# A feed-forward layer behind window attention on one core: the second layer of two blocks as seven block products, with the sums of w_out made on chip

## The chip, the core and the metric

The kernel runs on one core of a Trainium2 chip. A core has TensorE (PE in the profile, its weight loads PEld), which multiplies matrices from SBUF into the eight banks of PSUM, VectorE (DVE), ScalarE (ACT) and GpSimd (POOL) for work on elements, and SyncE (SP), which here only issues DMAs; ScalarE and GpSimd issue DMAs too. Each engine works off its own list of instructions in order and waits on semaphores for the others. The metric is the time of one execution in microseconds of device time, the median of the runs.

## The reference

Attention with a causal window of 64 keys, and behind it a feed-forward layer with a leaky rectifier. All is float32.

```python
# q, k, v: (8, 8, 576, 64); w_in: (512, 2048); w_out: (2048, 512)
scores = scale * np.matmul(q, k.transpose(0, 1, 3, 2))
mask = (rel >= 0) & (rel < window)
scores = np.where(mask, scores, -1000000000.0)
attn = np.exp(scores - np.max(scores, axis=-1, keepdims=True))
attn = attn / (np.sum(attn, axis=-1, keepdims=True) + 1e-09)
x = np.matmul(attn, v)          # then laid out as (4608 tokens, 512)
h = x @ w_in
g = np.maximum(0.01 * h, h)
return g @ w_out
```

## The kernel before

The 4608 tokens are nine chunks of 512. The first three are done beside the attention in the plain way: h = x w_in in blocks of 128 columns (L853), g, and g w_out into accumulators (L862). The other six are three blocks, s = 0, 1, 2, of two chunks (t = 0, 1) each. To keep float32's precision, each operand is split into a high part that TensorE takes as it is and the remainder (the low part), and a product is three matmuls: high by high, high by low, low by high.

The first layer of a block (L1006, tiles m) is done as a 2 x 2 scheme of seven products in place of eight (a Strassen-like scheme): sums and differences of x (made by `x_build`, L788) by sums and differences of w_in (made once by the loop at L935: fetch two single-precision pieces from DRAM, four sums on VectorE, a split, two stores to `w_first` in DRAM). For each of 8 values of f there are seven products of 6 matmuls; VectorE and ScalarE put them together into four parts of g (L1012 to L1018). The second layer (L1031, tiles y) is the plain product: for each t and each of 16 f, ScalarE and VectorE split g into a pair of tiles (L1021, L1024; 512 columns, four pairs in rotation) and TensorE does four output tiles i by three matmuls of 512 columns into four PSUM banks, o0 to o3: 2 x 16 x 4 x 3 = 384 matmuls a block. `put_out` (L1033) evicts the banks, and SyncE stores them.

The weights of both layers come from DRAM by `fill` (L991), a GpSimd DMA of 1 MB into one of four ring tiles, which is issued when TensorE has left the tile. Late attention (`attend` and `normalise`, L734 and L758) goes on beside block 0 and the beginning of block 1: scores (L267), mask (L648), maximum across partitions on GpSimd (L657), subtraction (L664), exponential (L668), sum on GpSimd (L660), values (L704). The pairs of units are numbered m, 16 of them late (m from 20).

The order of each engine's instructions is decided at build time by a planner, `arrange` (L519): each step has a duration, the steps that it waits for, and a rank, and on each engine the step of lowest rank that is ready goes next. The numbers in it are the author's estimates; only the order that comes out reaches the chip. The first part of the program, up to some 130 us, is in an order written out by hand (L52); it also converts the 64-bit weights to single precision (L194 to L240) and stores the pieces of w_in (`split`, L232) for the preparation.

Buffer names in the profile: p, pfew, pxa, pxb are SBUF places that are used again and again, gs is a pair of tiles for the split g, e, late_e and late_f hold scores in rotation, g (as a VectorE operand of L664) the maxima, late_o the sums.

Of the kernel before, what the change touches and what calls it, by code (L numbers as in the profile page):

```python
# [24 lines left out]
P = 128  # L25
# [57 lines left out]
RING_AT = (5, 6, 7, 8)  # L83
KT = DM // P
# [14 lines left out]
def band_attention_ffn(ctx: ExitStack, tc: tile.TileContext, qT, kB, vW, vL, w_in, w_out, eye_mask, out, outT):  # L99
# [24 lines left out]
    vs = [const.tile([P, UNITS, 544], F32, name="v")]  # L124
    unit = const.tile([P, P], F32R, name="unit")
# [20 lines left out]
    def v_of(m):  # L146
        if m >= PAIRED:
            return vs[0][:, :, : H * D]
        return vs[m % 2 if m < TURNED // 2 else 0][:, :, : H * (D + 1)]
# [35 lines left out]
    w_single = dram.tile([FT, P, 512], F32, name="w_single")  # L185
    w_first = dram.tile([P, half * 7 * 512], F32, name="w_first")
    w_second = dram.tile([half, P, 2, 1024], F32, name="w_second")
# [45 lines left out]
    def split(n):  # L233
        nc.scalar.copy(flat(parts(n)[0]), singles[n])
        if n % 2 == 0:
            nc.scalar.dma_start(w_single[n // 2], singles[n])
# [159 lines left out]
    def open_room():  # L396

        e, n, f = (wk.tile([P, 512, 2], U32, tag="raw", bufs=3, name=f"late_{x}") for x in "enf")
# [175 lines left out]
    def g_part(t, f):  # L574
        n = 2 * t + f // half
        return g_tile(f % half)[:, 512 * n : 512 * (n + 1)]
# [50 lines left out]
    for f in turn_of:  # L627
# [4 lines left out]
        to = w_second[f // 2, :, f % 2].rearrange("p (i c) -> p i c", i=2)  # L632
        stored.append((f, partial(store, to, f, slice(None), slice(2, 4))))
# [8 lines left out]
    def shield_of(m, j):  # L642
# [4 lines left out]
        e, s = (x.rearrange("a (b c) -> a b c", c=n * QB) for x in (e_of(m)[:, j], ps))  # L647
        nc.vector.scalar_tensor_tensor(e, s, SCALE, a, ALU.mult, ALU.add)  # L648

# [12 lines left out]
    def minus_of(m, j):  # L662
        e = e_of(m)[:, j]
        nc.vector.tensor_tensor(e, e, most_of(j), ALU.subtract)  # L664
# [7 lines left out]

    def inverse_of(m):
        c = later["c"][m % 2]
        nc.vector.tensor_scalar_add(c, c, 1e-9)
# [58 lines left out]
    def attend(m, gate):  # L734
# [8 lines left out]
        takes = [before["take"], two["take"]] if m == EARLY else ()  # L743
# [3 lines left out]
        )  # L747
        for j in range(2):
            o[f"E{j}"] = op("DVE", ONE, partial(shield_of, m, j), o["S"], three.get("V"), three.get(f"A{j}"), gate, before.get("E1"), rank=0.8 + late)
        for j in range(2):  # L750
            o[f"P{j}"] = op("POOL", 1.95, partial(max_of, m, j), o[f"E{j}"], before.get(f"B{j}"), rank=0.5 + late)
            o[f"B{j}"] = op("DVE", TWO, partial(minus_of, m, j), o[f"P{j}"], rank=0.8 + late)
# [5 lines left out]
    def normalise(m):  # L758
# [3 lines left out]
        if "v" in o and before:  # L762
            o["v"]["after"].append(before["V"])
        o["I"] = op("DVE", 0.4, partial(inverse_of, m), o["c0"], o["c1"], rank=0.8 + late, lag=0.3 + 6 * late)
# [23 lines left out]
    def x_build(s, n, xt_at, xt_free, x_free):  # L788

        urge = 1.0 if s else 0.2  # L790
        m = (UPC * LEAD + 2 * UPC * s) // UNITS + 2 * n

        def raw():
            return g_tile(xt_at[0])[:, :1024].rearrange("p (i q c) -> p i q c", i=2, q=4)

        def sums():
            return g_tile(xt_at[1])[:, 1024 * (s == 0) :][:, :1024].rearrange("p (k i c) -> p k i c", k=4, i=2)
# [4 lines left out]
        def fetch(i):  # L802
            nc.sync.dma_start(g_tile(xt_at[0])[:, 512 * i : 512 * (i + 1)], x_rows[m + i])
# [6 lines left out]
        d = op("DVE", 0.5, partial(sub, 4, 0, 2), *got, rank=urge, lag=3 * urge - 0.4)  # L810
        d3 = op("DVE", 0.5, partial(sub, 6, 1, 0), *got, rank=urge, lag=3 * urge - 0.4)
# [14 lines left out]
        for a, b, after in ((0, 2, got), (2, 3, got), (3, 7, [d, d2, d3, d4])):  # L826
            hi = op("ACT", 0.2 + 0.213 * (b - a), lambda a=a, b=b: nc.scalar.copy(x_view(0, a, b), source(a, b)), *after, *x_free, rank=urge, lag=3 * urge - 0.4)
# [107 lines left out]
    for f in range(half):  # L935
        def prep(i, f=f):
            return g_tile(PREP_AT + f % 2).rearrange("p (k i c) -> p k i c", k=4, i=2)[:, :, i]
# [240 lines left out]
```

## Time and profile before

| | us |
|---|---|
| median of 3 runs | 879.53 (879.51 to 881.62) |
| the profiled execution | 879.38 |
| its span, first to last instruction | 877.6 |

TensorE is busy all the time. By stages, from the timeline: the attention with the first three chunks to about 338 us; block 0, first layer to 433 and second to 535; block 1, first layer to 623 and second to 710; block 2, first layer to 786 and second to 873. Block 0 and the first layer of block 1 are longer because attention's matmuls lie among theirs. A profile row of instructions gives the line, engine, operation, the tile written and those read, shapes and count, then busy time and mean duration, then the engine's idle time just ahead of them and what ended it.

### The profile page before, as it was taken

To read this page: it belongs to the slowest core of one execution; us is meant where nothing else is said; L and a number is where in the kernel's file an instruction comes from. 1 tells how busy PE (TensorE), PEld (TensorE's weight loads), DVE (VectorE), ACT (ScalarE), POOL (GpSimd) and SP (SyncE) were. 2 spreads that over 40 slices of the span, in tenths; PEclk is the share of its full clock that TensorE was granted. 3 is DMA by queue.
4 is the path that set the end of the run, shared out by engine and by line. 5 is a ranking of instruction groups with operands and counts; after the bars stand their busy time and mean duration, and the time that the engine had idled before them with its cause. 6 is when DMAs were issued, how large, how long until landed. Compare 5 with 4: busy or idle time off the path is not lost.

```text
span 877.6 us, 16928 instructions
## 1 busy us (share of the span) xinstructions
PE 866.8 (99%) x6874; PEld 702.3 (80%) x6874; DVE 548.5 (63%) x843; ACT 329.7 (38%) x560; POOL 364.1 (41%) x222
## 2 busy tenths in 40 slices
PE   9999999999999998999999999999999999999998
PEld 5787888888878786887888887788888888888886
DVE  7999776657669976976677767664346324332321
ACT  4666544333323443433424332433334223332221
POOL 5332002969877513696874678850000000000000
PEclk9999999999999999999999999999999999999999
DMA  9774857576998697898799799877578575655661
GB/s 339 244 249 133 269 163 267 179 253 201 280 300 305 228 334 257 300 320 263 247 289 322 251 297 298 283 233 240 193 254 264 196 244 193 194 196 198 208 227 64
DMA packets 82557, 214.49 MB, mean 244 GB/s; under 512 B 16048, under 2 KB 26416, under 8 KB 70960
## 3 DMA queue, kind: packets, MB, share of 16 engines
q0 software_dynamic: 12960, 94.38, 32.6%
q10 hardware_dynamic: 28400, 60.53, 20.9%
q1 hardware_dynamic: 41120, 58.51, 20.3%
q8 instruction: 54, 0.88, 0.4%
q14 instruction: 23, 0.19, 0.1%
HBM read 168.59 MB, written 44.68 MB: 243 GB/s over the span
## 4 chain that ended last, share of the span: by engine, by line
PE 82%; DMA 7%; DVE 6%; issue 2%; ACT 1%; SPq 1%; ACTq 0%; POOL 0%; DVEq 0%; POOLq 0%
PE y L1031 30%; PE m L1006 25%; PE h L420 5%; PE acc L456 5%; PE h L853 5%; PE acc L862 4%; PE s L267 3%; PE o L704 2%; DMA rows<-late_c 2%; DMA late_c<-late_o 1%; DMA late_r<-rows 1%; PE o L356 1%; DMA p<-x_rows 1%; DMA raw<-w_out 1%; DMA w_second<-p 1%
## 5 line engine op out<-in xcount | busy, mean ns | idle before, releaser
L1006 PE MATMUL m<-pfew,p 128*128 128x512 f32 x720 | 171.3, 392 | 0.6 <-DVE pfew L830 0.4
L1006 PEld LDWEIGHTS m<-pfew,p 128*128 128x128 f32 x720 | 133.9, 188 | 30.1 <-DVE pxa L1015 1.1
L1031 PE MATMUL y<-pxa,p 128*128 128x512 f32 x576 | 136.8, 391 | 0.0
L1031 PE MATMUL y<-gs,p 128*128 128x512 f32 x576 | 135.4, 390 | 0.0
L1031 PEld LDWEIGHTS y<-gs,p 128*128 128x128 f32 x576 | 107.9, 188 | 22.6
L1031 PEld LDWEIGHTS y<-pxa,p 128*128 128x128 f32 x576 | 107.5, 188 | 22.6
L993 POOL DMA_DIRECT2D p<-w_second x48 | 25.6, 533 | 174.3 <-PE y L1031 131.6
L862 PE MATMUL acc<-p,gs 128*128 128x512 f32 x324 | 79.6, 393 | 0.0
L1018 ACT ACTIVATE p<-p 128x512 f32<-128x512 f32 x63 | 39.8, 632 | 105.9 <-DVE p L1015 100.7
L657 POOL PARTITION_ALL_REDUCE g<-late_f x20 | 36.8, 1874 | 101.5 <-DVE late_f L648 101.5
L1006 PE MATMUL m<-pxb,p 128*128 128x512 f32 x288 | 71.5, 393 | 2.2 <-DVE p L1015 1.2
L660 POOL PARTITION_ALL_REDUCE late_o<-late_f x20 | 65.7, 3299 | 15.2 <-ACT late_f L668 6.9
L1015 DVE TENSOR_TENSOR p<-m,pxa 128x512 f32<-128x512 f32 x63 | 43.3, 687 | 45.3 <-PE m L1006 44.9
L862 PEld LDWEIGHTS acc<-p,gs 128*128 128x128 f32 x324 | 60.0, 188 | 12.9
L1024 DVE TENSOR_TENSOR gs<-p,gs 128x512 fp32r<-128x512 f32 x48 | 36.9, 772 | 53.2 <-ACT gs L1021 53.2
L1015 DVE TENSOR_TENSOR pxa<-m,pxa 128x512 f32<-128x512 f32 x57 | 39.2, 689 | 49.5 <-PE m L1006 48.0
L993 POOL DMA_DIRECT2D p<-w_first x42 | 22.7, 541 | 113.3 <-PE m L1006 65.6
L660 POOL PARTITION_ALL_REDUCE late_o<-late_e x18 | 61.6, 3442 | 11.1 <-issue 5.0
L1006 PEld LDWEIGHTS m<-pxb,p 128*128 128x128 f32 x288 | 53.4, 188 | 15.0 <-DVE p L1015 1.6
L660 POOL PARTITION_ALL_REDUCE late_o<-e x18 | 58.9, 3303 | 6.0 <-ACT e L668 4.1
L1021 ACT CAST gs<-p 128x512 fp32r<-128x512 f32 x48 | 29.9, 622 | 74.1 <-PE y L1031 73.9
L853 PE MATMUL h<-pxa,p 128*128 128x512 f32 x228 | 56.2, 393 | 0.9 <-DVE gs L873 0.9
(139 smaller groups left out, 1335.3 us busy)
## 6 DMA issues: line engine op xcount, KB each, us to landing
p<-w_second POOLq DMA_DIRECT2D x48, 1024.0 KB, 5.2
p<-w_first POOLq DMA_DIRECT2D x42, 1024.0 KB, 5.8
v<-vL ACTq DMA_DIRECT2D x27, 512.0 KB, 5.6
raw<-w_out ACTq DMA_DIRECT2D x15, 512.0 KB, 4.1
k<-kB ACTq DMA_DIRECT2D x28, 256.0 KB, 4.5
raw<-w_in ACTq DMA_DIRECT2D x14, 512.0 KB, 4.1
late_r<-rows SPq DMA_DIRECT2D x56, 128.0 KB, 5.7
q<-qT ACTq DMA_DIRECT2D x26, 256.0 KB, 5.1
```

The lines of the kernel that those rows point to most:

```text
L420: nc.tensor.matmul(ps, a[:, k, :], b[:, k, part], start=n == 0, stop=n == len(terms) - 1)
L456: nc.tensor.matmul(acc[c, i], a[:, ts], b, start=begin and n == 0, stop=end and n == 2)
L657: nc.gpsimd.partition_all_reduce(most_of(j), e_of(m)[:, j], P, ReduceOp.max)
L660: nc.gpsimd.partition_all_reduce(sum_of(j), e_of(m)[:, j], P, ReduceOp.add)
L853: nc.tensor.matmul(ps, a[:, k, :], b[:, k], start=i == 0, stop=i == len(terms) - 1)
L862: nc.tensor.matmul(acc[c, i], a[:, i * P : (i + 1) * P], b, start=begin and k == 0, stop=n in ends and k == 2)
L993: nc.gpsimd.dma_start(ring[n], of)
L1006: nc.tensor.matmul(tiles[b], w[:, 256 * i + 128 * kt : 256 * i + 128 * kt + 128], x_part(OF_X[k], j, kt), start=begin and c == 0, stop=c = ...
L1015: nc.vector.tensor_tensor(to(), tiles[b], x(), ALU.add)
L1018: nc.scalar.activation(to(), to() if b is None else tiles[b], AF.Prelu, alpha=0.01)
L1024: nc.vector.tensor_tensor(g_pair(q)[1], x(), g_pair(q)[0].bitcast(F32), ALU.subtract)
L1031: nc.tensor.matmul(tiles[i], a, b, start=f == 0 and k == 0, stop=f == FT - 1 and k == 2)
```

## The change

Four things are changed.

1. In blocks 1 and 2 the second layer is done as seven products too. The outputs are halves t (two chunks) by halves of the output columns, and the inner dimension is halved: f below and from 8. A product k runs over 8 values of f and two output tiles, three matmuls each, into two banks: 7 x 8 x 2 x 3 = 336 matmuls. Its weights are those of slot 0 to 7 of `w_second`, its factor is g or a sum of parts of g, which `combine` forms in place, in pieces of 1024 columns (two f). `wide_high` and `wide_low` split such a piece into a pair of tiles; three pairs are in rotation (`pairs_of_g`, a new pair `third`, and the place that U has in the first layer). Products are kept and added up in SBUF places that attention has left (q, k, late_o) and stored from there. `x_build` for block 2 uses places that attention has left, since g stays in use longer. Banks in block 2 are turned by two.
2. The sums of w_out that slots 1, 3, 5 and 7 need are made on chip by `prepare(1, f)`, with a third place `spare` for both kinds of preparation; `split` stores the single pieces of w_out to DRAM as well as those of w_in. `w_second` has another layout, and the stores to it are in two halves.
3. For the pairs from m = 20 the masked scores are written back into their PSUM bank (L657), ScalarE copies them to SBUF for the maximum (L663), and VectorE subtracts the maximum from the scores in PSUM (L679). The next pair's scores wait for these subtractions. The `1e-9` is added by ScalarE (`guard_of`) in place of VectorE, and odd late pairs have a place of their own for the values (`more_v`).
4. GpSimd's DMA scratch in SBUF is 4 KB a partition; it wasn't set before. `spare` takes 8 KB and `more_v` 4 KB a partition.

```diff
+HELD_FROM = 20
+IN_PREP_AT = (0, 0, 0, 6, 7, 0, 6, 7)
+OUT_PREP = 1.0
+IN_SEVEN = (1, 2)
...
+    more_v = const.tile([P, UNITS, 512], F32, name="more_v")
...
-    w_second = dram.tile([half, P, 2, 1024], F32, name="w_second")
+    w_second = dram.tile([P, 8 * half * 512], F32, name="w_second")
+    second_at = w_second.rearrange("p (k f c) -> p k f c", k=8, f=half)
...
     def split(n):
         nc.scalar.copy(flat(parts(n)[0]), singles[n])
-        if n % 2 == 0:
-            nc.scalar.dma_start(w_single[n // 2], singles[n])
+        nc.scalar.dma_start(w_single[n], singles[n])
...
     def minus_of(m, j):
         e = e_of(m)[:, j]
-        nc.vector.tensor_tensor(e, e, most_of(j), ALU.subtract)
+        nc.vector.tensor_tensor(e, probs[m][j] if held_back(m) else e, most_of(j), ALU.subtract)
...
+        if held_back(m - 1) and before:
+            takes += [before["B0"], before["B1"]]
...
+            o[f"C{j}"] = op("ACT", ACTS, partial(copy_of, m, j), o[f"E{j}"], *free, rank=0.5 + late) if held else o[f"E{j}"]
...
+    used_last = {PREP_AT + i: slot_free[14 + i] for i in range(2)}
+    used_last[0] = []
+    for f, n in enumerate(IN_PREP_AT):
+        prepare(0, f, n, 0.4 + 0.15 * f, *used_last[n])
+        used_last[n] = prepared[0, f]
+    for f in range(half):
+        prepare(1, f, 0, OUT_PREP + 0.1 * f, *used_last[0])
+        used_last[0] = prepared[1, f]
...
+    FACTORS = ((0, 0, 0), (1, 0, 0), (2, 0, 1), (3, 1, 0), (5, 1, 0), (4, 0, 1), (7, 1, 1))
+    BANK_OF = (0, 2, 0, 2, 0, 2, 0)
...
+    def wide_high(s, n, t, j, p):
+        nc.scalar.copy(wide_pair(s, n)[0], quarter(t, j, p))
+
+    def wide_low(s, n, t, j, p):
+        hi, lo = wide_pair(s, n)
+        nc.vector.tensor_tensor(lo, quarter(t, j, p), hi.bitcast(F32), ALU.subtract)
+
+    def combine(p, to, a, b, how):
+        nc.vector.tensor_tensor(quarter(*to, p), quarter(*a, p), quarter(*b, p), how)
+
+    def seventh(s, k, f, n, pair):
+        b, begin = bank_at(s, BANK_OF[k]), k not in (2, 5, 6)
...
+        gh, gl = (x[:, 512 * (f % 2) :][:, :512] for x in wide_pair(s, pair))
+        for i in range(2):
+            wh, wl = (ring[n][:, 512 * (f % 4) + 256 * a + P * i :][:, :P] for a in range(2))
+            for c, (a, x) in enumerate(((wh, gh), (wh, gl), (wl, gh))):
+                nc.tensor.matmul(
+                    tiles[b + i], a, x, start=begin and f == 0 and c == 0, stop=f == half - 1 and c == 2,
+                    skip_group_check=not begin,
+                )
...
+    def second_in_seven(s):
...
+        for k, (slot, t, j) in enumerate(FACTORS):
+            b = bank_at(s, BANK_OF[k])
+            for p in range(4):
+                n = 4 * k + p
...
+                hi = op("ACT", HIGH, partial(wide_high, s, n, t, j, p), *ready_of, *free, rank=0.2)
+                split[k, p] = op("DVE", WIDE, partial(wide_low, s, n, t, j, p), hi, rank=0.2)
+                if p % 2 == 0:
+                    made_before = [y for f in range(half) for y in prepared[1, f]] if slot % 2 else []
+                    q, got = filled(w_second[:, 512 * (half * slot + 2 * p) :][:, :2048], *made_before)
+                for f in (2 * p, 2 * p + 1):
+                    after = bank_free[b] + bank_free[b + 1] if f == 0 else ()
+                    next_main(6 * MM, partial(seventh, s, k, f, q, n), got, split[k, p], *after)
+                tile_free[q % RING] = [main]
+                wide_free[n % 3] = [main]
...
+        if s in IN_SEVEN:
+            second_in_seven(s)
+            continue
...
-    nc = bacc.Bacc("TRN2", target_bir_lowering=False, num_devices=1)
+    nc = bacc.Bacc("TRN2", target_bir_lowering=False, num_devices=1, dynamic_dma_scratch_size=4096)
```

TensorE at the beginning of block 1's second layer, before (m is a tile of the first layer, y one of the second with t and i behind it, gs a split pair, the last name the ring tile):

```order
L1006 MATMUL m_7_3_6260<-pxb_3361,p_31_3567 128x512 x6
L1031 MATMUL y_0_0_6292<-gs_80,p_28_3422 128x512 x3
L1031 MATMUL y_0_1_6298<-gs_80,p_28_3422 128x512 x3
L1031 MATMUL y_0_2_6304<-gs_80,p_28_3422 128x512 x3
L1031 MATMUL y_0_3_6310<-gs_80,p_28_3422 128x512 x3
```

and with the change, at the third pair of the first product (z is a tile of a product, with its number and the output tile i behind it):

```order
L1121 MATMUL z_0_1_6458<-third_6190,p_29_3497 128x512
L1121 MATMUL z_0_0_6457<-pxa_40_6467,p_30_3547 128x512 x3
L1121 MATMUL z_0_1_6458<-pxa_40_6467,p_30_3547 128x512 x3
L1121 MATMUL z_0_0_6457<-pxa_40_6467,p_30_3547 128x512 x3
L1121 MATMUL z_0_1_6458<-pxa_40_6467,p_30_3547 128x512 x3
L1121 MATMUL z_0_0_6457<-gs_81,p_30_3547 128x512
```

A split of g of 512 columns served four tiles of three matmuls; one of 1024 columns now serves two tiles for each of two f.

VectorE in the same layer, before (L1024 splits g, L808 and L830 are the x build for block 2, L1034 evicts):

```order
L830 TENSOR_TENSOR pfew_3381<-p_33_3627,pfew_3381 128x4x256
L1024 TENSOR_TENSOR pxa_39_6302<-p_22_2842,pxa_39_6302 128x512
L808 TENSOR_TENSOR pxa_35_3675<-p_34_3671 128x256
L808 TENSOR_TENSOR pxa_35_3675<-p_34_3671,pxa_35_3675 128x256 x2
L1024 TENSOR_TENSOR gs_80<-p_32_3621,gs_80 128x512
L830 TENSOR_TENSOR pxb_3361<-p_34_3671,pxb_3361 128x2x256
```

and with the change, in the second and third product (L1107 splits, L1110 sums g in place, L857 is the x build, L1133 adds up a product):

```order
L1110 TENSOR_TENSOR p_36_3811<-p_36_3811 128x1024
L1107 TENSOR_TENSOR gs_82<-p_37_4079,gs_81 128x1024
L1133 TENSOR_TENSOR q_83<-z_1_0_6530,q_83 128x512
L1133 TENSOR_TENSOR q_84<-z_1_1_6531,q_84 128x512
L1110 TENSOR_TENSOR p_37_4079<-p_37_4079 128x1024
L1107 TENSOR_TENSOR third_6191<-p_26_3088,third_6190 128x1024
L1107 TENSOR_TENSOR pxa_40_6467<-p_24_2971,pxa_40_6467 128x1024
L1110 TENSOR_TENSOR p_26_3088<-p_26_3088 128x1024
```

Between the splits stand sums of the same width and the additions of a finished product; the x build stands among them as before.

ScalarE in the hand-written part, where the weights are converted, before (L234 casts a piece to its high part, L236 stores it, L199 fetches the next raw piece):

```order
L199 DMA raw_804<-w_out 128x1024
L234 CAST pfew_86<-w_756 128x512
L234 CAST pfew_86<-w_792 128x512
L236 DMA w_single<-w_792 128x512
L425 ACTIVATE g<-h_3_0_772 128x512
```

and with the change:

```order
L205 DMA raw_808<-w_out 128x1024
L240 CAST pfew_87<-w_760 128x512
L241 DMA w_single<-w_760 128x512
L240 CAST pfew_87<-w_796 128x512
L241 DMA w_single<-w_796 128x512
L430 ACTIVATE g<-h_3_0_776 128x512
```

The pieces of w_out (here w_760) are stored behind their cast too; the rest of that list is as it was.

More of the change, by code (lines that the diff above doesn't have):

```diff
@@ L1035, in put_out, with wide_pair @@
         nc.sync.dma_start(outT[s, i * P : (i + 1) * P, t], o())
+    FACTORS = ((0, 0, 0), (1, 0, 0), (2, 0, 1), (3, 1, 0), (5, 1, 0), (4, 0, 1), (7, 1, 1))
+    BANK_OF = (0, 2, 0, 2, 0, 2, 0)
+    def wide_pair(s, n):
+        if n % 3 == 0:
+            return [flat(x) for x in pairs_of_g]
+        if n % 3 == 2:
+            x = own(("g", s), F32R).rearrange("p f i c -> p (f i c)")
+            return x[:, :1024], x[:, 1024:]
+        if "third" not in held:
+            held["third"] = [wk.tile([P, 1024], F32R, tag="raw", bufs=3, name=f"third{i}") for i in range(2)]
+        return held["third"]
```

235 lines of the change are left out of this document (170 added, 65 removed).

## The prediction

> **What bounds the kernel now.** I read the page first, then the busy time by stretches, the chain of waits, and TensorE's timeline at the few places where it stands still.
>
> ```profile
> PE 866.8 (99%) x6874; PEld 702.3 (80%) x6874; DVE 548.5 (63%) x843; ACT 329.7 (38%) x560; POOL 364.1 (41%) x222
> PEclk9999999999999999999999999999999999999999
> 225.00:300.00 75.00, 75.00 (x754) 60.61 (x754) 59.77 (x78) 24.02 (x41) 59.10 (x22) 1.00 0.85 283
> 300.00:350.00 50.00, 46.83 (x313) 36.79 (x311) 33.28 (x54) 21.32 (x36) 9.38 (x8) 1.00 0.87 298
> 623.00:710.00 87.00, 87.00 (x386) 72.03 (x385) 38.02 (x63) 28.14 (x47) 8.44 (x16) 1.00 0.69 228
> 786.00:877.60 91.60, 87.47 (x386) 72.08 (x385) 24.04 (x35) 21.85 (x36) 6.86 (x13) 1.00 0.52 172
> ...
> 623.23 87.04 PE y L1031 x384
> 710.27 76.16 PE m L1006 x336
> 786.43 87.05 PE y L1031 x384
> ```
>
> The first two lines are the page's: TensorE (PE) is busy 99% of the span, at a granted clock of full speed throughout. The four rows of stretches give span, then busy time of PE, weight loads, VectorE, ScalarE and GpSimd, then clock, share of the DMA engines and GB/s. The last three rows are the end of the chain of waits: from 623.23 us to the last matmul at 873.48 it is one engine, without a gap. Those are the stages the change shortens: the second layer of blocks s = 1 and s = 2, 384 matmuls each. The chain gives the price of a matmul: 87.05 / 384 = **0.2267 us**; the 336 of the first layer cost the same (76.16 / 336). So these stages are set by the number of matmuls, as long as every operand arrives in time.
>
> Since busy PE time is modelled, I check it against the weight loads.
>
> ```profile
> L1031 PEld LDWEIGHTS y<-gs,p 128*128 128x128 f32 x576 | 107.9, 188 | 22.6
> ```
>
> A load takes 188 ns of each 226.7 ns period, so 83% is the most that loads can reach at this shape; 72.03 us of 87.00 is 83%. The stage is full. [...]
>
> **The change part by part.** *The second layer.* Seven products of a 2 x 2 scheme, each 8 blocks x 2 output tiles x 3 terms, are 336 matmuls, where there were 384. Two blocks lose 2 x 48 = 96 matmuls: 96 x 0.2267 = **-21.8 us**. The form is unchanged (128 x 128 weights, 512 columns), so the price is.
>
> *What must keep up with it.* VectorE and ScalarE now split g in pieces of 1024 columns, form sums of g in place and add the products up. The nearest rows (name, shapes, count, then busy us and mean ns of one) are from the same stages:
>
> ```profile
> L830 DVE TENSOR_TENSOR pfew<-p,pfew 128x1024 fp32r<-128x1024 f32 x2 | 2.5, 1226 | 0.4 <-ACT pfew L827 0.4
> L1024 DVE TENSOR_TENSOR gs<-p,gs 128x512 fp32r<-128x512 f32 x30 | 20.8, 692 | 45.4 <-ACT gs L1021 45.4
> L808 DVE TENSOR_TENSOR p<-p,p 128x256 f32<-128x256 f32 x4 | 1.7, 422 | 0.1
> L827 ACT CAST pfew<-p 128x1024 fp32r<-128x1024 f32 x2 | 2.1, 1048 | 0.0
> L830 DVE TENSOR_TENSOR pfew<-pxa,pfew 128x1024 fp32r<-128x1024 f32 x2 | 3.3, 1660 | 0.0
> ```
>
> In the order after the change VectorE has, from the first to the last matmul of this stage in s = 1: 26 splits, 11 sums and 4 pieces of the x build at 1.226 us (41 x 1.226 = 50.3), 14 operations of 512 columns at 0.692 (9.7) and 12 of 256 at 0.422 (5.1): **65.0 us** for a PE stage of 336 x 0.2267 = 76.2. Per product (10.9 us of PE) that is 9 to 10.5 us in the six first ones and 5 in the last. In s = 2, without the x build, it is 53. ScalarE has 39. So VectorE keeps up, at 85%, with little to spare. The latency is covered too: three pairs of split tiles are in rotation, a pair is used for 12 matmuls (2.72 us), so after its release there are 5.4 us for one cast (1.05), one VectorE operation ahead in the queue (1.23) and the split (1.23), 3.5 in all. I take **0**. If the wide operations took 1.66 us, as the last row shows for two of them while GpSimd was reducing, the sum would be 65.0 + 41 x 0.434 = 82.8, 6.6 us over the stage; below zero there is nothing to gain. I stay with 1.226, since GpSimd does nothing but issue DMAs there (8.44 us busy in the third stretch).
>
> *The weights.* A fill of 1 MB serves 24 matmuls, 5.44 us, before and after.
>
> ```profile
> q0 software_dynamic: 12960, 94.38, 32.6%
> p<-w_second POOLq DMA_DIRECT2D x48, 1024.0 KB, 5.2
> p<-w_first POOLq DMA_DIRECT2D x42, 1024.0 KB, 5.8
> L993 POOL DMA_DIRECT2D p<-w_second x48 | 25.6, 533 | 174.3 <-PE y L1031 131.6
> ```
>
> Four ring tiles let three fills run ahead, 16 us for a landing of 5.2 to 5.8: **0**, unless the smaller scratch takes this overlap away (rival A).
>
> *Sums of w_out on chip.* Eight preparations more (12 MB of DMA, and on VectorE 8 x (4 x 0.422 + 1.226) = 23 us), and 16 stores of 256 KB more from the conversion of the weights. Most of the preparations lie in block 0 and have until the second product of s = 1. In the order, the last store of them stands some 230 matmuls (50 us) ahead of the first fill that reads one. But three preparations more than before are finished ahead of the first layer of s = 0, which waits as it is:
>
> ```profile
> 301.66 1.67 PE L853 MATMUL h<-pxa,p 128*128 128x512 f32 x6 [0.87 <-DVE gs L873]
> 338.60 0.47 PE L1006 MATMUL m<-pxb,p 128*128 128x512 f32 x1 [0.29 <-issue]
> 339.49 1.42 PE L1006 MATMUL m<-pxb,p 128*128 128x512 f32 x5 [0.42 <-DVE pxb L830]
> 341.56 7.18 PE L1006 MATMUL m<-pfew,p 128*128 128x512 f32 x29 [0.41 <-DVE pfew L830]
> 349.90 3.00 PE L1006 MATMUL m<-pxb,p 128*128 128x512 f32 x12 [1.16 <-DVE p L1015]
> ...
> 296.25 3.27 DMA late_c<-late_o
> 311.22 6.35 DMA rows<-late_c
> 318.15 5.83 DMA late_r<-rows
> 324.80 4.68 DMA x_rows<-late_n
> 329.49 7.29 DMA p<-x_rows
> ```
>
> The first rows are PE's timeline with its idle time in brackets, 3.2 us in these five. The others are the chain of waits behind them: five DMAs one after another, 27.4 us, bring the last normalised heads to the first product, with the DMA engines 0.85 to 0.87 busy. Three preparations of 1.5 MB are 4.5 MB more, beside the 33 MB that the first fence's rates (283 and 298 GB/s) move from 225 to 340 us, about an eighth. If these legs grew by an eighth, they would cost 3.4 us; the best case is that the waits vanish (-3.2), because the last values stand 12 matmuls earlier in the order. I take **+1.0**, nearer the rows that already wait.
>
> The other stores stand behind the ScalarE cast of each w_out piece. Their buffer rotates with two, so the next join but one must wait for the landing:
>
> ```profile
>   DMA w_single<-w: 0.7, 2
> ...
> 0.00:130.00 130.00, 127.05 (x1257) 100.38 (x1258) 113.55 (x234) 77.00 (x138) 31.94 (x20) 1.00 0.72 236
> ...
> DMA to landing us min/median/max: 2.0/4.3/7.4
> ```
>
> That is what the 16 stores before cost VectorE: 0.7 us in two waits. Twice as many stores cost it about 0.7 more, though it is busy 113.55 of these 130 us. PE is idle for 2.95 us of them, mostly ahead of its first operands; I take **0** between 0 and 0.7.
>
> *Late scores in PSUM.* The masked scores of the last 16 pairs are written back into their bank, ScalarE copies them (0.58 us, as its copy in the last fence below), and VectorE subtracts the maximum from PSUM.
>
> ```profile
> L664 DVE TENSOR_TENSOR late_f<-late_f,g 128x512 f32<-128x512 f32 x10 | 13.5, 1354 | 1.8 <-POOL g L657 1.8
> L715 DVE TENSOR_TENSOR late_n<-o,late_r 128x512 f32<-128x512 f32 x16 | 10.8, 677 | 2.6 <-issue 2.2 <-DMA late_r<-rows 0.4
> L660 POOL PARTITION_ALL_REDUCE late_o<-late_f x20 | 65.7, 3299 | 15.2 <-ACT late_f L668 6.9
> L657 POOL PARTITION_ALL_REDUCE g<-late_f x20 | 36.8, 1874 | 101.5 <-DVE late_f L648 101.5
> ...
> 367.58 1.09 PE s L267 x64
> ...
> 382.51 1.09 PE s L267 x64
> ```
>
> An operation with one PSUM operand takes 0.677 beside a busy GpSimd, one with two SBUF operands 1.354: 32 x 0.68 = 22 us less on VectorE. It isn't on the path, so that is worth 0. The new wait is that the next scores need the bank: masks 2 x 0.68, a copy 0.58, two maxima 3.75, a subtraction 0.68, 6.4 us, while scores follow each other by 14.9 us, with 51 to 54 main matmuls between them in both orders. Behind a waiting score on PE stands the main layer itself. No in-place operation on PSUM by VectorE is in the trace; between 0.68 and 1.35 it fits: **0**.
>
> *The end.* Where four tiles were evicted by two engines, two are now added by VectorE.
>
> ```profile
> 872.83 0.69 DVE L1034 COPY p<-y 128x512 f32<-128x512 f32 x1 [0.67 <-PE y L1031]
> 873.51 0.58 ACT L1034 COPY p<-y 128x512 f32<-128x512 f32 x1 [0.77 <-PE y L1031]
> ```
>
> The last tile's 0.58 becomes 0.69: **+0.1**.
>
> *Sum*, against the profiled execution's own time, 879.4 (span 877.6 and 1.8 around it; the median of the runs, 879.5, is the same): 879.4 - 21.8 + 1.0 + 0.1 = **858.7 us**.
>
> **Rivals.** *A, slower: GpSimd's fills lose their overlap in the 4 KB scratch.* If the next fill could only be issued when the last has landed, its period would be 0.53 + 5.8 = 6.33 us in the first layer, 0.53 + 5.2 = 5.73 in the second, against 5.44. Blocks 1 and 2 have 28 fills of each: 28 x 0.89 + 28 x 0.29 = +33.0, so 858.7 + 33.0 = **891.7**. It turns to slower than before from 5.44 + 20.7 / 56 = 5.81 us a fill. For it: nothing shows how much scratch a fill takes. Against it: q0 has 12960 / 90 = 144 packets a fill, few things to keep. [...]
>
> *B: VectorE sets the pace of the second layer in s = 1* with wide operations at 1.66 us: +6.6, **865.3**. For it: 10.5 of 10.9 us in two products. Against it: 1.226 in every such row after 623 us.
>
> *C: the first layer of s = 0 starts late* by a fifth on the five DMA legs, +5.5 in place of +1.0: **863.2**.
>
> *D: scores wait for their bank* because the two sums of the pair before (2 x 3.30) run ahead of the maxima: 6.4 + 6.6 = 13.0 of 14.9 us, and queues on three engines add 2.4 more; half a microsecond over in each of 16 is +8: **866.7**.
>
> *E: it doesn't shorten the stages,* because the product's operands arrive too late all along: 76.2 stays 87, about **879**. Nothing but a mistake of mine on the rotation speaks for it.
>
> **How the numbers follow.** The forecast has 0.64, A 0.06, B 0.10, C 0.11, D 0.05, E 0.04. The range runs from 854.5 (the waits before the first layer gone, 858.7 - 4.2) to 865.5, which takes in B and C; A, D and E are left out (0.15), and some of the forecast's own tails. A measurement of this kernel can tell 0.3%, 2.6 us, from no change. Faster by more than that are the forecast, B, C and D (0.90); the same is E (0.04); slower is A (0.06).
>
> **What would show it.** In the changed profile two second layers of 76.2 us must stand in the chain, each without idle time on PE; VectorE's wide groups at 1.23 us; fills landing in 5 to 6 us with GpSimd waiting for PE and not for the ring; scores with no wait for a subtraction; and 2 to 5 us of idle time around the first product of s = 0. The prediction is wrong if PE waits for a split (B), for a fill (A) or for scores (D) by more than 2 us in total, or if the first layer of s = 0 starts more than 3 us later.

## The result, and the profile after

The changed kernel takes 888.38 us (median of 15 runs, 883.05 to 891.85) where the kernel before takes 880.93 (15 runs, 878.59 to 883.99): a ratio of 1.0079, with a 95% interval of 1.0057 to 1.0100. It is 0.8% slower. The forecast was 858.7; neither its range nor its sign held. The profiled execution took 888.97 us, 887.2 of them its span. All times and ratios here and below are of undisturbed executions; e5, e8 and e11 each had one slow one, which is left out.

The page after gives engines and TensorE's granted clock; the last rows are the end of its chain of waits (start, us, what).

```profile
PE 853.5 (96%) x6778; PEld 690.0 (78%) x6778; DVE 631.6 (71%) x891; ACT 376.0 (42%) x620; POOL 364.2 (41%) x218
PEclk9999999999999998999999999989999999999999
...
654.58 76.16 PE z L1121 x336
730.74 76.16 PE m L1058 x336
806.90 76.17 PE z L1121 x336
```

The part that the change is about works as it should. Each second layer (tile z) is one piece of 336 matmuls and 76.16 us, 0.2267 us each, in place of 87.05. The clock row shows two slices below 9, where before had none. So the loss lies ahead of 654.58 us. The next two fences cut that time at the first matmul of each stage (block 0's first layer, its second, block 1's first, block 1's second), before and after; columns are those of the prediction's stretches: span, busy time of PE, weight loads, VectorE, ScalarE and GpSimd, then clock, share of the DMA engines, GB/s.

```profile
0.00:338.60 338.60, 334.49 (x3242) 268.11 (x3243) 258.11 (x433) 154.91 (x272) 157.67 (x72) 1.00 0.76 251
338.60:433.80 95.20, 93.19 (x913) 74.31 (x914) 73.66 (x98) 35.33 (x58) 70.77 (x40) 1.00 0.85 281
433.80:535.80 102.00, 101.67 (x929) 82.21 (x927) 78.30 (x104) 34.27 (x58) 69.12 (x41) 1.00 0.87 282
535.80:623.10 87.30, 87.06 (x689) 70.64 (x690) 47.92 (x72) 29.94 (x50) 43.83 (x28) 1.00 0.80 258
```

```profile
0.00:357.40 357.40, 338.59 (x3242) 269.99 (x3242) 271.33 (x445) 161.44 (x290) 157.18 (x72) 0.99 0.81 269
357.40:448.90 91.50, 91.50 (x920) 74.70 (x913) 64.38 (x93) 43.25 (x76) 70.09 (x39) 1.00 0.94 306
448.90:562.90 114.00, 109.02 (x1058) 87.24 (x1057) 95.83 (x116) 46.25 (x84) 83.93 (x45) 0.97 0.93 291
562.90:654.40 91.50, 85.73 (x560) 69.08 (x561) 51.99 (x77) 32.05 (x57) 32.41 (x24) 0.96 0.78 254
654.40:730.60 76.20, 76.20 (x338) 63.08 (x337) 61.12 (x67) 37.20 (x44) 7.40 (x14) 1.00 0.71 228
```

Block 1's second layer starts at 654.4 in place of 623.1, 31.3 us late. Of these, 18.8 are lost before the first product of block 0, with the same 3242 matmuls, and 12.5 in the three stages behind it. TensorE stands idle for 29.6 us up to there (span less busy), where it was 6.7; the other 8.4 us are longer busy time, since the granted clock is below 1 in three stages (0.99, 0.97 and 0.96). Five waits of TensorE (line, released by, total, times, longest) hold most of it:

```profile
PE h L880 <- DVE gs L900: 7.4, 2, 5.9
PE m L1058 <- ACT p L1070: 5.0, 1, 5.0
PE y L1083 <- issue: 3.8, 1, 3.8
PE s L306 <- DVE pxb L395: 3.4, 2, 2.1
PE s L272 <- issue: 1.9, 1, 1.9
```

Two waits lead back to transfers. The rows below are from three views of the changed kernel: the chain of waits around the longest one (start, us, what), SyncE's timeline there, and the chain ahead of the wait of 5.0 us, which ends at 580.68.

```profile
321.19 13.34 DMA w_second<-p
...
334.55 0.33 ACTq L992
...
335.99 0.59 ACT gs L897
...
336.60 0.70 DVE gs L900
...
337.35 5.43 PE h L880 x12
```

```profile
320.71 1.35 SPq L632 DMA_DIRECT2D w_second<-p  x2
324.39 0.33 SPq L697 DMA_DIRECT2D rows<-late_c  x1
...
335.32 1.49 SPq L710 DMA_DIRECT2D late_r<-rows  x2
```

```profile
552.88 9.69 DMA w_second<-pspare
562.56 6.69 DMA late_r<-rows
...
569.41 9.16 DMA outT<-p
...
578.59 0.34 ACTq L165
```

A store to `w_second` takes 13.34 us to land; ScalarE's queue stands at an issue (L992), and behind it stands the cast (L897) for which VectorE and TensorE wait. The issue moves other data than that store. What ties them is the completion semaphore: SyncE's and ScalarE's DMAs (465 before, 529 after) share eight, and in the traces of both kernels none is issued before the last one on its semaphore has landed. The waits of ScalarE's queue that end with such a landing sum up to 12.0 us before and 54.3 after, 45.8 of them behind SyncE's transfers; no run changes them by themselves. The 4 KB of `rows` leave SyncE at 324.39, right behind two such stores, and are read from 335.32 on, 10.9 us later. At 580 us it is a store of a preparation (`pspare`), then two more transfers, then a load that ScalarE has to issue (L165) before it reaches what TensorE waits for; L165 too waits for the landing ahead of it (`outT`, 578.57) by the semaphore alone. In both places an engine that issues DMAs in its own order holds back work for TensorE while transfers are slow. The wait of 3.8 us, at 507.10, is of another kind: it ends when VectorE has evicted a bank (L1086, from 506.32), which stood behind 2.98 us of the x build (L857). The question for the runs is which transfers, and why there.

### The profile page after: what moved, and what is told of

Its sections match the earlier page's. It is cut to its first block, busy times and chain, and to the rows that moved or that the text cites. A ratio compares the mean times of both kernels' runs of the same rounds, so it can differ in the third digit from the quotient of the medians.

```text
span 887.2 us, 16927 instructions
## 1 busy us (share of the span) xinstructions
PE 853.5 (96%) x6778; PEld 690.0 (78%) x6778; DVE 631.6 (71%) x891; ACT 376.0 (42%) x620; POOL 364.2 (41%) x218
## 4 chain that ended last, share of the span: by engine, by line
PE 48%; DMA 12%; DVE 9%; issue 3%; ACT 1%; SPq 1%; ACTq 0%; POOL 0%; DVEq 0%
PE m L1058 25%; PE z L1121 17%; DMA w_second<-p 2%; DMA late_r<-rows 2%; DMA w_second<-pspare 2%; DMA rows<-late_c 2%; DMA x_rows<-late_n 1%; PE y L1083 1%; PE acc L889 1%; DMA p<-x_rows 1%; PE s L272 1%; PE o L722 1%; DMA outT<-p 1%; DVE p L835 1%; DVE gs L1076 1%
## 5 line engine op out<-in xcount | busy, mean ns | idle before, releaser
L1067 DVE TENSOR_TENSOR p<-m,pxa 128x512 f32<-128x512 f32 x60 | 41.3, 688 | 41.9 <-PE m L1058 41.6
L1067 DVE TENSOR_TENSOR pxa<-m,pxa 128x512 f32<-128x512 f32 x60 | 41.3, 689 | 41.0 <-PE m L1058 38.0
L880 PE MATMUL h<-pxa,p 128*128 128x512 f32 x228 | 58.4, 405 | 5.9 <-DVE gs L900 5.9
L675 POOL PARTITION_ALL_REDUCE late_o<-late_e x18 | 58.9, 3292 | 12.5 <-ACT late_e L683 8.0
L1121 PE MATMUL z<-gs,p 128*128 128x512 f32 x240 | 57.6, 389 | 0.0
L880 PEld LDWEIGHTS h<-pxa,p 128*128 128x128 f32 x228 | 43.9, 195 | 16.5 <-DVE gs L900 7.2
L1083 PE MATMUL y<-gs,p 128*128 128x512 f32 x192 | 48.7, 406 | 3.8 <-issue 3.8
L1121 PEld LDWEIGHTS z<-gs,p 128*128 128x128 f32 x240 | 45.0, 188 | 9.4
L1121 PE MATMUL z<-third,p 128*128 128x512 f32 x216 | 51.9, 389 | 0.0
L1121 PE MATMUL z<-pxa,p 128*128 128x512 f32 x216 | 51.9, 389 | 0.0
```

The costliest lines, as they stand in the source:

```text
L675: nc.gpsimd.partition_all_reduce(sum_of(j), e_of(m)[:, j], P, ReduceOp.add)
L880: nc.tensor.matmul(ps, a[:, k, :], b[:, k], start=i == 0, stop=i == len(terms) - 1)
L1067: nc.vector.tensor_tensor(to(), tiles[b], x(), ALU.add)
L1083: nc.tensor.matmul(tiles[i], a, b, start=f == 0 and k == 0, stop=f == FT - 1 and k == 2)
L1121: nc.tensor.matmul(tiles[b + i], a, x, start=begin and f == 0 and c == 0, stop=f == half - 1 and c == 2, skip_group_check=not begin,)
```

## The experiments

Fifteen kernels, each timed beside the kernel before on the same chip. "Ratio" is to that run of the kernel before (880.55 to 882.28 us in these runs). Each has one profile, of a single execution; those of the changed family can lie up to 7 us from their median (e13 ran in 863.16 to 874.07 us in six executions), so a small difference between two profiles shows little.

| run | what | us | ratio, 95% interval |
|---|---|---|---|
| after | | 888.38 | 1.0079, 1.0057 to 1.0100 |
| e1 | after, bytes of w_out preparations / 8 | 880.97 | 0.9994, 0.9971 to 1.0018 |
| e2 | e1, and bytes of the added stores / 8 | 880.47 | 0.9991, 0.9967 to 1.0015 |
| e3 | after, late scores in SBUF | 880.41 | 0.9990, 0.9967 to 1.0014 |
| e4 | before, 4 KB scratch | 880.62 | 1.0003, 0.9987 to 1.0020 |
| e5 | after, stores at 3 a step | 885.37 | 1.0037, 1.0014 to 1.0060 |
| e6 | before, stores halved | 888.64 | 1.0076, 1.0053 to 1.0099 |
| e7 | e5 and e2 | 874.10 | 0.9905, 0.9880 to 0.9929 |
| e8 | e5, guard on VectorE | 881.71 | 1.0000, 0.9975 to 1.0025 |
| e9 | e5, w_in preparations later | 874.33 | 0.9913, 0.9884 to 0.9942 |
| e10 | e8 and e9 | 870.07 | 0.9869, 0.9844 to 0.9894 |
| e11 | after, w_in preparations later | 883.83 | 1.0024, 0.9997 to 1.0052 |
| e12 | e10 and e2, but for one preparation and two stores | 862.45 | 0.9782, 0.9755 to 0.9808 |
| e13 | e10, four places for the pieces | 869.04 | 0.9867, 0.9828 to 0.9906 |
| e14 | e10, late scores in SBUF | 875.86 | 0.9943, 0.9922 to 0.9964 |
| e15 | e13, late scores in SBUF | 873.77 | 0.9924, 0.9908 to 0.9941 |

The theories at the start are T1, the added bytes, and three rivals: T2, the added steps in ScalarE's queue and its order; T3, the 4 KB scratch; T4, the conversion of the weights, held up by the added stores. T5 to T7 came from what the first runs showed.

**e1 and e2: fewer bytes.** All instructions stay in their order; fetches and stores carry an eighth. The fills of the slots with sums read other slots in their place, so these kernels (e7 and e12 too) multiply by other weights.

```diff
-            nc.scalar.dma_start(to, w_single[2 * (f + half * i) + n].rearrange("p (k c) -> p k c", k=2))
+            of = w_single[2 * (f + half * i) + n].rearrange("p (k c) -> p k c", k=2)
+            some = 32 if n else 256
+            nc.scalar.dma_start(to[:, :, :some], of[:, :, :some])
...
-                nc.scalar.dma_start(second_at[:, 1::2, f, 256 * i : 256 * i + 256], prep(i))
+                nc.scalar.dma_start(second_at[:, 1::2, f, 256 * i : 256 * i + 32], prep(i)[:, :, :32])
```

> After, with every instruction kept in its place on its engine, but the fetches and stores of the eight preparations of w_out cut to an eighth of their columns (10.5 MB less to move between 225 and 600 us; the fills of slots 1, 3, 5 and 7 read slots 0, 2, 4 and 6 instead, so those products use other weights). Theory T1 (the preparations' bytes fill the DMA engines, 0.92 to 1.00 busy from 225 to 580 us, so loads that an in-order queue waits for land later): the waits of TensorE at 337 (5.9 us), 507 (3.8) and 580 us (5.0) shrink to less than half and the time falls by 12 to 22 us, to 866 to 876. Theory T2 (the added ScalarE work and the order in which its queue has copies, guards and issues): the waits stay, 885 to 891. T4 (the conversion of the weights): only the loss ahead of 130 us, some 5 us, is its, and stays here.

> As e1, and the 16 stores of single w_out pieces behind the conversion cut to an eighth too (3.7 MB less ahead of some 170 us). T4 (these stores make the conversion of the weights late, by the joins that wait for their landing and by the raw loads beside them): TensorE's idle time ahead of 130 us falls from 8.1 us to near the 3.0 of before, and the time by 4 to 5 us against e1. T1 alone: within 2 us of e1.

e1 is 7.4 us below after, too little for T1 and more than T2 allowed. Block 0's second layer and block 1's first get shorter (205.5 to 197.2 us together, by their first matmuls), but the wait of 5.9 us ahead of block 0 stays, as 5.83, and its first product starts at 360.9. So the bytes of the preparations are a part of the loss, behind block 0's start; what is lost ahead of it has another cause. e2 is e1 within the interval.

**e3 and e4: the scores and the scratch.** `HELD_FROM = 100` in after; `dynamic_dma_scratch_size=4096` in before.

> After, with the masked late scores written to SBUF as before (no copy by ScalarE, the subtraction from SBUF, no wait of the next scores for it); the planner makes a new order. T2 (the copies and the held bank are what holds TensorE): the waits at 507 and 580 us go, 872 to 880. T1: the traffic is the same, so 884 to 892, with waits of the same sum at the same or other places.

> Before, with GpSimd's DMA scratch at 4 KB and nothing else. T3 (the small scratch makes the fills late or slower): slower than before by over 3 us, and fills that land later than 5.2 and 5.8 us or wait at their issue. T1, T2 and T4: no difference, within 1.5 us of before.

e4 is before within 0.2%: the scratch costs nothing, rival A falls. e3 fell between the two theories; its profile, of an execution of 885.86 us, 5.4 above its median, still has long waits (9.6, 3.2 and 2.6 us lead its list). e14 and e15 take it up again.

**e5 to e7: the pace of the stores.** The rows of SyncE's queue named the cause that no theory had so far. The stores of the resident weights (the list `stored`, issued at L632) are handed out two at each step of the first three chunks. The change made two stores of each one to `w_second`, so that the list has 56 in place of 40, and left the pace. The last one of before, of after, of e5 and of e6 leaves SyncE at:

```profile
261.19 0.46 SPq L624 DMA_DIRECT2D w_second<-p  x1
```

```profile
320.71 1.35 SPq L632 DMA_DIRECT2D w_second<-p  x2
```

```profile
262.63 0.94 SPq L632 DMA_DIRECT2D w_second<-p  x2
```

```profile
312.51 1.00 SPq L624 DMA_DIRECT2D w_second<-p  x2
```

e5 changes one number, `PACE = 2` to `PACE = 3`; e7 does so with the edits of e2; e6 halves the stores in the kernel before:

```diff
-        to = w_second[f // 2, :, f % 2].rearrange("p (i c) -> p i c", i=2)
-        stored.append((f, partial(store, to, f, slice(None), slice(2, 4))))
+        for a in range(2):
+            to = w_second[f // 2, :, f % 2].rearrange("p (i c) -> p i c", i=2)[:, :, 256 * a : 256 * a + 256]
+            stored.append((f, partial(store, to, f, slice(None), slice(2, 4), slice(256 * a, 256 * a + 256))))
```

> After, with the stores of the resident weights handed to SyncE three at each step of the first three chunks in place of two (PACE = 3). New theory T5: the change halved each w_second store, so there are 56 such stores in place of 40, and at two a step the last leave SyncE at 322 us in place of 261; their landing (13.3 us) stands ahead of the small transfers that bring the last normalised heads, and frees the places for x late. By T5 the last of these stores leaves by 275 us, the wait of 5.9 us at 337 us goes, the first layer of s = 0 starts at 343 to 348 us in place of 357.4, and the time falls by 8 to 14 us, to 874 to 881. T1 (volume of the preparations alone): the same bytes are moved, so within 3 us of after, 885 to 892.

> Before, with each store to w_second in two halves of 256 KB (40 stores become 56, the same bytes) and PACE = 2, nothing else. T5: the last of them leaves SyncE after 310 us, and the first layer of s = 0 starts 6 to 14 us later than at 338.6; the time is 886 to 895, near after. T1: no difference, within 2 us of before.

> After with PACE = 3, and the preparations of w_out and the 16 added stores of single pieces cut to an eighth of their columns, as in e2 (14 MB less). If the loss is the pace of the stores and the added bytes together and nothing else, the sum of the prediction comes out: 857 to 864. If something else holds TensorE (the ScalarE queue, the scores held in PSUM), 866 or more.

e6 settles that the halved stores at the old pace are a cause by themselves: with no byte more and nothing else, they make the kernel before 0.76% slower (0.53 to 0.99%), and its block 0 starts at 346.8 in place of 338.6. It does not tell the pace from the number or the size of the stores; e9 against e11, below, does. In e5 the 5.9 us wait is gone, but block 0 starts at 352.8, not at 343 to 348, and the gain is 3.0 us, hardly clear of noise, not 8 to 14. e7, 874.1, is 10 us above the upper end of what the pace and the bytes together would leave. Something else holds TensorE back between 200 and 300 us, where e5 has five waits (7.5 us) and before has none.

**e8 to e11: the guard, and preparations that start early.** The changed kernel has a third place for preparations that is free from the start, so the four preparations of w_in that it gets no longer wait for the last weights to leave their places. The first sums of a preparation stand in VectorE's timeline, in before, after and e9, at:

```profile
258.54 2.82 DVE L946 TENSOR_TENSOR p<-p 128x256 f32<-128x256 f32 x4
```

```profile
161.58 3.68 DVE L979 TENSOR_TENSOR pspare<-pspare 128x256 f32<-128x256 f32 x4
```

```profile
262.08 2.82 DVE L979 TENSOR_TENSOR p<-p 128x256 f32<-128x256 f32 x4
```

The edits are the guard as it was in before (`tensor_scalar_add` by VectorE, no ScalarE step), and

```diff
-IN_PREP_AT = (0, 0, 0, 6, 7, 0, 6, 7)
+IN_PREP_AT = (6, 7, 6, 7, 6, 7, 6, 7)
...
+    used_last[0] = prepared[0, half - 1]
     for f in range(half):
         prepare(1, f, 0, OUT_PREP + 0.1 * f, *used_last[0])
```

> e5 (after with PACE = 3), and the 1e-9 added by VectorE right ahead of its reciprocal as before, with no instruction on ScalarE. Theory T6: the guard on ScalarE waits for the transfer of the sums (5.10 us at 241.9 in e7) at the head of ScalarE's queue, and the exponentials and leaky rectifiers behind it wait too, while VectorE waits for the guard; PE's waits at 204, 228, 246, 268 and 289 us in e5 (7.3 us together, none of which is in before) are its. By T6 four of these five go, the main matmul 1020 of the first three chunks starts at 299 to 304 us in place of 309.9, and the time falls 5 to 10 us below e5, to 875 to 881. T7 (the preparations of w_in, three of which may now start early and share VectorE with attention): within 2 us of e5.

> e5, and the preparations of w_in in the two places of before alone (not before the last weights have left them), those of w_out in the third place behind them. T7: the waits between 200 and 300 us go, 875 to 881. T6: they stay, within 3 us of e5; the preparations of w_out then stand later, beside block 0's second layer, and may cost 1 to 3 us there.

> Both edits. If T6 and T7 add up, 5 us below the better of e8 and e9; by T6 alone within 3 us of e8. To come near the 858.7 of the sum it would have to lose the traffic of the w_out preparations as well, which is still there: not below 864.

> After (PACE = 2, guard on ScalarE), with only the preparations of w_in in the two places of before and those of w_out behind them, as in e9. If early preparations (T7) and the pace of the stores (T5) are costs of their own: 876 to 883, some 9 to 12 us below after, and the last store to w_second still leaves SyncE after 305 us, with a wait of 4 us or more between 320 and 350 us or the first layer of s = 0 4 to 8 us later than the 341.7 of e9. If T7 alone is the cause and the pace matters only in the order of before: within 2 us of e9, 872 to 876.

T7 holds: e9 is 11.0 us below e5. Of its waits between 200 and 300 us only one of 1.0 us is left, and block 0 starts at 341.7. What the early preparations displaced is seen in the stretch from 130 to 230 us of before, e5 and e9:

```profile
130.00:230.00 100.00, 100.00 (x1036) 80.92 (x1039) 64.99 (x84) 37.67 (x67) 69.25 (x28) 1.00 0.68 221
```

```profile
130.00:230.00 100.00, 97.42 (x941) 78.63 (x941) 69.82 (x89) 37.41 (x67) 57.73 (x23) 1.00 0.83 277
```

```profile
130.00:230.00 100.00, 100.00 (x981) 81.07 (x980) 65.73 (x79) 38.42 (x73) 64.67 (x27) 1.00 0.74 240
```

In e5 VectorE does 5 us more there and the DMA engines move a quarter more, and GpSimd, which only attention uses in this stretch, gets 11.5 us less of its work done; attention is then late for the values and the heads that TensorE needs (4.4 us of e5's waits between 200 and 300 us are ahead of values, for VectorE). The runs move a preparation as a whole, and with it the first ones of w_out, so whether VectorE's time, the bytes or ScalarE's issues count more stays open.

T6 is not shown. In e8 TensorE's waits from 200 to 300 us sum up to 7.7 us, in e5 to 7.5, at other places. e8 is 3.7 us below e5 and e10 4.3 below e9, but the intervals overlap both times.

e11 has the early preparations cured and the pace not: its last store leaves at 321.20 us, block 0 starts at 349.9, and it is only 4.5 us below after, where costs of their own would have given 9 to 12. So each cure alone gives little (3.0 and 4.5 us), both together 14.1 (e9). e9 and e11 differ in `PACE` alone, with the same stores, and are 9.5 us apart (intervals 0.9884 to 0.9942 and 0.9997 to 1.0052): that shows the pace itself as a cause. A likely reading is that as long as one of the two keeps the last heads late, the other has nothing to shorten.

**e12: the bytes that are left.**

> e10, with seven of the eight preparations of w_out and 14 of the added stores of single pieces cut to an eighth of their columns, some 12 MB less, every instruction kept (those products use other weights). This is the price that the bytes still have in e10: if they are what is left, 857 to 863, with TensorE ahead of the first main matmul 240 at 91.5 us in place of 93.5; if what is left is not the bytes but the waits of an order with more in it, within 3 us of e10, 867 to 873.

e12 is 7.6 us below e10, as e1 was 7.4 below after. The stretch of block 0's second layer, in e10 and in e12:

```profile
437.10:548.80 111.70, 105.72 (x1057) 85.13 (x1055) 96.07 (x126) 46.29 (x79) 80.74 (x45) 1.00 1.01 324
```

```profile
434.20:541.20 107.00, 105.20 (x1058) 85.25 (x1056) 94.05 (x126) 47.39 (x79) 81.87 (x45) 1.00 0.95 299
```

The share of the DMA engines is 1.01 in e10. At 0.95 the same work has 1.8 us of idle time in place of 6.0. The main matmul 240 of the first three chunks, expected at 91.5 us, stayed at 93.3.

**e13: the joins.** The pieces of the conversion rotate through the four quarters of `spare` in place of two places.

```diff
-        singles[n] = wk.tile([P, 512], F32, tag="o", name=f"w{n}")
+        singles[n] = spare[:, 512 * (n % 4) :][:, :512]
```

> e10, with the single-precision pieces of the conversion in the four quarters of the place spare, which nothing uses until the conversion is done, in place of two places in rotation; all bytes and stores stay, and so does the order. T4 in the form of the joins: every kernel of the changed family reaches the main matmul 240 of the first three chunks 2 to 5.5 us later than before (93.5 in e10, 89.5 in before), and in e12 it was still 93.3 though the stores had an eighth of the bytes, with a join that waited 3.1 us for the landing of one. If the landing that frees a place is the cause, the join waits for no w_single store any more, the main matmul 240 is reached by 89.5 to 91.5 us, and the time falls 2 to 4 us, to 866 to 868. If the traffic beside the raw loads is, 92.5 to 94 us and within 1.5 us of e10.

VectorE's waits ahead of 130 us, in e12 and in e13:

```profile
DVE w L237 <- DMA w_single<-w: 3.1, 1, 3.1
```

```profile
DVE raw L221 <- DMA raw<-w_in: 2.0, 2, 1.6
DVE raw L221 <- DMA raw<-w_out: 1.4, 2, 0.9
```

The join's wait was there with an eighth of the bytes and is gone with four places. The main matmul 240 comes at 91.7 us (93.5 in e10, 89.5 before), a little beyond the bound of the expectation. The nine profiles with all these stores and two places have it at 92.2 to 95.9, and e15, with four places, at 91.4, so some of the delay went with the joins. The rest may be the wait for the raw loads, 3.4 us here and 1.2 before; no run shows it. The time, 1.0 us below e10, can't be told from it.

**e14 and e15: the scores once more.**

> e10, with the late scores in SBUF as before (the edit of e3). e3 came out 8 us below after, between what T2 and T1 said (880.4; 872 to 880 and 884 to 892). If the scores in PSUM cost by themselves (the copies in ScalarE's queue, the bank that the next scores wait for), the same edit on e10 brings 4 us or more: 862 to 866, with block 0's second layer at 109 us or less in place of 111.7. If e3's gain came from the order that the planner happened to make, or from less crowding in an order that e10 has cleared already: within 2.5 us of e10, or slower.

> e13, with the same edit. If the scores in PSUM cost by themselves: 861 to 865 and below e13 by about as much as e14 is below e10. If not: within 2.5 us of e13's 869.0, and the differences of e14 and e15 to their bases need not agree in sign.

The same edit that made after 8.0 us faster makes e10 5.8 and e13 4.7 us slower. So e3's gain was not a price of the scores in PSUM, and what made it stays open; with the other causes out of the way the scores in PSUM, with the order that the planner makes for them, save some 5 us. The subtraction (busy us, mean ns) in e10 and in e14, one of three groups each:

```profile
L679 DVE TENSOR_TENSOR e<-s,g 128x512 f32<-128x512 f32 x10 | 6.8, 682 | 2.3 <-POOL g L672 2.2
```

```profile
L679 DVE TENSOR_TENSOR e<-e,g 128x512 f32<-128x512 f32 x10 | 10.1, 1022 | 2.3 <-POOL g L672 2.3
```

All three groups are 21.8 us in e10 and 31.7 in e14. How much of the 5 us comes from these 10 us and how much from the other order isn't told apart.

e10, 870.07 us, and e13, 869.04, beat both kernels: 1.3% faster than before.

## Why the prediction was wrong

**The second layer, -21.8:** right. Two stages of 76.16 us stand where 87.05 stood, without idle time on TensorE.

**VectorE and ScalarE keep up, 0:** right. The wide groups take 1.22 us, and VectorE is busy 61.12 of the 76.20 us (the working had 65.0):

```profile
L1107 DVE TENSOR_TENSOR gs<-p,gs 128x1024 fp32r<-128x1024 f32 x9 | 11.0, 1223 | 2.8 <-ACT gs L1103 2.8
L1110 DVE TENSOR_TENSOR p<-p,p 128x1024 f32<-128x1024 f32 x5 | 6.1, 1221 | 0.1
```

Rivals B and E fell with it. **The fills, 0:** right; those of w_second land in 5.3 us (5.2 before), those of w_first in 6.1 (5.8), and e4 shows the scratch at nothing.

**The first layer of s = 0, +1.0 between -3.2 and +3.4:** this step failed; it measured +18.8. Of these, 5.5 are lost by the main matmul 240 already (95.0 us in place of 89.5), where the added stores are, below. Its place was named (rival C), its price was not. It priced three early preparations by their bytes in five transfers, an eighth more, and left two things out. The halving of the w_second stores was read as a change of layout and given no term at all, though the pace at which they are handed out is by count; e6 shows it to cost the kernel before 7.0 us, and e9 against e11 shows 9.5 for the pace. And the early preparations were taken as traffic beside the last heads at 300 us, while their sums start at 161.58 and displace attention from there on; e9 against e5 shows 11.0. The two prices don't add: without both, e9 is 14.1 below the changed kernel.

**Sums of w_out on chip, 0:** failed. The step looked at when the sums are needed, and that is 50 us later than they are made. But the price isn't lateness of the sums: the bytes go through a stretch where the DMA engines were 0.85 to 0.87 busy already, and without them the stages there get shorter. They cost 7.4 us (e1), 7.6 (e12) and, with the bytes of the added stores, 11.3 (e5 to e7).

**The 16 added stores, 0 between 0 and 0.7:** mis-sized where they stand. In the changed kernel the joins wait for their landing 3.1 us in place of 0.7:

```profile
DVE w L237 <- DMA w_single<-w: 3.1, 3, 1.9
```

The raw loads are waited for 4.9 us in place of 1.2, and the main matmul 240 comes 2.7 to 6.4 us later than before in the nine profiles named at e13. In the time it isn't shown: e2 lies 0.5 below e1 and e13 1.0 below e10, within the intervals.

**Late scores in PSUM, 0:** the working was right that no score waits long for its bank (rival D fell; 1.2 us in the changed kernel), but wrong that less work on VectorE beside the path is worth nothing. With the path cleared it is worth some 5 us together with the order that it brings (e14, e15). VectorE saves 10 us by it and not 22: the working took the dearest of three groups of before (1354 ns; the others take 1216 and 1159).

**The guard** was given no term, and the runs don't tell it from nothing.

From the forecast to the measured time the runs make these steps: 858.7 forecast, 3.8 left over in e12, of which the cause stays open, 7.6 for the bytes of the preparations and stores (e12 to e10), 18.3 for the pace, the early preparations and the guard (e10 to after): 888.4. The expected gain came in full and was given back ahead of the stages that made it.

## What to carry to other kernels

When a change splits an instruction, look for what counts instructions: a pace, a rotation, a planner's slots. A cost of nothing for an added transfer needs the share of the DMA engines in its stretch, and a look at what stands behind each in-order queue that issues or awaits a transfer there, and at which earlier transfer its next issue waits for. And a new buffer lets work start earlier, which is no gain when it starts beside work that the path needs first.

## What the runs showed of the hardware

After its three longest pauses TensorE came back at about half of its full clock in the changed kernel. Behind the waits of 5.91, 3.78 and 4.99 us (stretches as above):

```profile
337.30:342.80 5.50, 5.46 (x13) 4.33 (x14) 5.02 (x10) 3.05 (x5) 0.00 (x0) 0.52 0.71 272
...
507.00:514.00 7.00, 6.90 (x45) 5.37 (x46) 5.31 (x7) 1.17 (x2) 4.37 (x2) 0.55 1.00 303
580.60:587.00 6.40, 6.32 (x19) 5.08 (x20) 4.46 (x8) 3.91 (x8) 6.37 (x4) 0.66 0.58 164
```

5.5 us at 0.52, 7.0 at 0.55 and 6.4 at 0.66 lose 8.0 us, which is nearly the longer busy time of the first section (8.4): by this estimate each of these three waits costs 2.2 to 3.2 us more than it lasts. The clock of that trace is at 0.50 three times ahead of the last matmul, from 335.74, 506.41 and 578.09 us, each time from within one of these pauses, and for 6.83 us. In e9 shorter stretches of idle time were followed by 0.50 too: TensorE was idle for 1.10 us of the 8.90 up to 488.90, and for 1.97 of the next 2.90.

```profile
480.00:488.90 8.90, 7.80 (x71) 5.95 (x61) 8.81 (x12) 2.16 (x3) 4.39 (x3) 1.00 1.04 336
488.90:491.80 2.90, 0.93 (x3) 0.47 (x3) 0.98 (x1) 2.12 (x5) 1.44 (x1) 0.88 1.06 307
491.80:495.00 3.20, 3.16 (x8) 2.48 (x8) 3.20 (x6) 1.74 (x4) 3.20 (x2) 0.50 1.08 396
```

And the length of a pause alone doesn't decide in these runs. A pause of 3.0 us in e13 was not followed by half clock; the first row below is that wait, the second the stretch that has it, with a mean clock of 1.00 (0.999 over the whole execution):

```profile
PE m L1056 <- DVE p L1084: 3.0, 1, 3.0
...
340.00:636.00 296.00, 290.48 (x2631) 235.93 (x2630) 236.48 (x332) 132.22 (x216) 188.70 (x109) 1.00 0.95 313
```

How much idle time brings half clock, and what ends it, was not shown.
